# One column instead of sixteen products, first sums on TensorE, and a new order of loads and preparation pieces in an attention-and-FFN kernel

## The chip, the cores and the metric

The kernel runs on one core of one Trainium2 chip. The metric is the device time of one execution in microseconds. The kernel before took 1346.77 (median of 3 runs, 1346.31 to 1349.07).

## What is computed

A batch of 4 attentions over pooled keys, and a two-layer network on every token that comes out. The reference, cut:

```python
q: (4, 12288, 128) * 0.8;  kv: (4, 384, 32, 128) * 0.1;  w_sr: (128, 128)
kv_pool = kv.reshape(B, H//4, 4, W//4, 4, C).mean(axis=(2, 4))
k = v = kv_pool.reshape(B, -1, C) @ w_sr            # 768 keys per batch
a = softmax(q @ k.T / sqrt(C))
x = a @ v                                           # 49152 tokens
h = x @ w_in                                        # 128 -> 2048
out = (h - tanh(h)) @ w_out                         # 2048 -> 128
```

## The kernel before

The kernel uses that the softmax is close to uniform. With exp(s) - 1 - s as the small remainder of a score, the sum over keys is split into a straight part (products with the moment matrix Mh of the values) and the remainders' part. The network is expanded about the batch's centre: with h = h0 + d, h - tanh(h) is a value at h0, a slope times d, and terms of second and third order.

**Groups.** The 49152 tokens form 96 groups of 512 columns (24 groups a batch). `attention(g)` makes scores against 6 tiles of 128 keys, two at a time (L783, tile big), their exponentials (L787) and remainders r2 (L790, fp16, three tiles of 128x1024 a group). The three are summed: SP copies the first into rs (L802), POOL's two adding DMAs put the others on top (L805), and TensorE sums rs over the keys with a matrix of ones (`shares`, L809, into den). ACT turns this into the share t (L829). Numerator num: straight matmuls (L815) and values (L825). df = num * t (L836, DVE), its rounding dr (L839, POOL), the rest dl (L863, POOL). `feed_forward(g)` makes the 16 tiles of the first layer from dr (L894), on seven pairs ACT squares (L898) and DVE forms the cubes r (L901), on one pair ACT copies and POOL does the cubing (L905, L908, L912); `back` (L932) sums them with Wr, `straight` (L883) adds the slopes' product Ah, and ACT adds the value G0 as the bias (L943) and the result is stored.

**Preparation of a batch.** `keys(b)` makes pooled keys kvp: for batch 0 from 12 loads of 512 KB (L376) that DVE (L390) or POOL (L384) sum; for batches 1 to 3 by 16 DMAs, 15 of them adding DMAs of POOL (L362, "gather"), one for each group. Then the mean (row, L424 to L429), the centre (pc, L436, and col, L439), keys kTr, values vvr, the moment. `about_centre(b)` makes the first layer at the centre, four pieces `first(n)` of four matmuls (L535), the polynomial in hb (POOL for b > 0, DVE for b = 0), the scaled first-layer weights winr, `value(n)` (16 matmuls of one column, L595, summed into G0), `by_first(n)` (POOL, L697: output weights times slope) and `slopes(n)` (L701, 16 matmuls, summed into A, split into Ah), and `by_third(n)` (POOL, L714, weights Wr).

**Weights.** The weights arrive as 64-bit words. `words_of` loads 512 KB (L247 for w_in, L249 for w_out) and ACT (three operations) and DVE (four) turn them into 32 bits.

**What sets the order.** Every piece is an operation of `Plan` with a step, an engine, an estimated duration, and what it reads and writes. Plan.run places the operations one by one on the engine that is free first, smallest step first among those that can start; this is fixed when the program is built. Each engine, and SP's queue of loads, then runs its own list strictly in order. A name such as "held" that belongs to no tile only orders the planning; no semaphore comes of it. Steps are counted 8 to a group. The tables EARLY and LATER hold the steps between pieces of the preparation for batches 0 and 1 and for 2 and 3. Buffers per tag are in BUFS; the PSUM tags x (den, num and most of the preparation) and acc have one bank each, big three.

Of the kernel before, what the change touches and what calls it, by code (L numbers as in the profile page):

```python
# [11 lines left out]
F16 = mybir.dt.float16  # L12
# [144 lines left out]
def attention_then_ffn(ctx: ExitStack, tc: tile.TileContext, q, kv_by_key, kv_by_place, w_sr, w_in,  # L157
# [18 lines left out]

    BUFS = {"kc": 2, "kvp": 1, "kTr": 2, "vvr": 2, "Mn": 1, "Mh": 2, "A": 2, "Ah": 2, "Wg": 3, "Wr": 2,
            "winr": 2, "q": 4, "qr": 5, "ql": 2, "E": 2, "r2": 7, "rs": 3, "t": 2, "dl": 1, "df": 1, "dr": 2, "u": 3, "r": 4,
            "rp": 2, "v": 2, "z": 1, "o": 2, "row": 2, "col": 2, "G0": 2, "hb": 2, "W2": 1,
# [53 lines left out]
    def words_of(step, load_step, n, kind):  # L233
# [56 lines left out]
        plan.op(load_step, "SP", 0.5, load_words, (), (words,), late=2.0, dma=1.27)  # L290
# [8 lines left out]
    def weights(step, load_step, out_step, load_out):  # L299
# [3 lines left out]
        for n in range(NW):  # L303
            words_of(out_step + n / 8, load_out + n / 8, n, "o")
# [46 lines left out]
    def keys(b, s0):  # L351
# [17 lines left out]
        for j in range(0 if b else NK):  # L369
# [18 lines left out]
            else:  # L388
# [3 lines left out]
                plan.op(s, "DVE", 1.2, pool, (key,), ((kvp, j),))  # L392
# [8 lines left out]
        apart_by = (1, 6, 8, 8)[b]  # L401
# [98 lines left out]
    def about_centre(b, s0):  # L500

        cen, hb, G0, Am, Wr, winr = (f"{x}.{b}" for x in ("cen", "hb", "G0", "A", "Wr", "winr"))
        ph, pg, pa = (f"{x}.{b}" for x in ("ph", "pg", "pa"))
# [5 lines left out]
        sb(G0, "G0", [P, 1])  # L509
# [4 lines left out]
        FS, CS, AS, APART, SA, VA, TA, WI, WS = EARLY if b < 2 else LATER  # L514
# [4 lines left out]
        value_at = [known + VA + AS * n if b else n / 2 + VL for n in range(4)]  # L519
        third_at = [known + TA + AS * (n + 0.5) if b else n / 2 - THIRD for n in range(4)]  # L520
        for n in range(4):
            if b or n == 0:
                bank(f"{ph}.{n}", "x" if b else "acc", first_at[n])
            if b:
                bank(f"{pg}.{n}", "x", value_at[n])
                bank(f"{pa}.{n}", "x", slopes_at[n] + APART)
        if not b:
            bank(f"{pa}.0", "acc", slopes_at[0])
            bank(f"{pg}.0", "acc", value_at[0])
# [63 lines left out]
        def value(n):  # L593
            for f in range(4 * n, 4 * n + 4):
                PE.matmul(out=plan[f"{pg}.{n if b else 0}"][:, 0:1], lhsT=wout32[:, f],  # L595
                          rhs=x(3)[:, f : f + 1], start=(f % (4 if b else FT) == 0),
                          stop=(f % 4 == 3 and (b > 0 or n == 3)))

        def sum_value(n):
            if n:  # L600
                V.tensor_tensor(out=plan[G0], in0=plan[f"{pg}.{n}"][:, 0:1], in1=plan[G0], op=ALU.add)
            else:
                V.tensor_scalar(out=plan[G0], in0=plan[f"{pg}.{n}"][:, 0:1], scalar1=1.0,
                                scalar2=None, op0=ALU.mult)

# [20 lines left out]
        for n in range(4):  # L626
            plan.op(value_at[n], "PE", 0.9, partial(value, n), (gg, ("wout32", n)),
                    (f"{pg}.{n if b else 0}",), late=0.2)
            if b:
                plan.op(value_at[n], "DVE", 0.15, partial(sum_value, n), (f"{pg}.{n}",), (G0,))  # L630
        if not b:
            plan.op(value_at[3], "DVE", 0.15, partial(sum_value, 0), (f"{pg}.0",), (G0,))
# [28 lines left out]
        else:  # L661
            for j in range(2):
                pw = f"pw.{b}.{j}"
                big(pw, winr_at + j / 2)
                for k in range(2):
                    dg = f"dg.{b}.{j}.{k}"
                    sb(dg, "Wg", [P, FW, C], step=winr_at + j / 2 + k / 4)
                    fs = slice((2 * j + k) * FW, (2 * j + k + 1) * FW)

                    def diagonal(j=j, dg=dg, fs=fs):  # L670
                        by = x(8)[:, fs].unsqueeze(2).to_broadcast([P, FW, P])
                        of = ident.unsqueeze(1).to_broadcast([P, FW, P])
                        (PL if j else V).tensor_tensor(out=plan[dg], in0=of, in1=by, op=ALU.mult)

                    def scaled(j=j, k=k, dg=dg, pw=pw):
                        for n in range(FW):
                            f = (2 * j + k) * FW + n
                            at = (k * FW + n) * P
                            PE.matmul(out=plan[pw][:, at : at + P], lhsT=winT[:, f], rhs=plan[dg][:, n],
# [10 lines left out]
        for n in range(NW):  # L690
            wg = f"wg.{b}.{n}"
            fs = slice(n * FW, (n + 1) * FW)
            sb(wg, "Wg", [P, FW, C], step=slopes_at[n])

            def by_first(n=n, wg=wg, fs=fs):
                by = x(4)[:, fs].unsqueeze(2).to_broadcast([P, FW, C])
                PL.tensor_tensor(out=plan[wg], in0=wout32[:, fs], in1=by, op=ALU.mult)  # L697

            def slopes(n=n, wg=wg):
                for k in range(FW):  # L700
                    PE.matmul(out=plan[f"{pa}.{n if b else 0}"][:, 0:P], lhsT=winT[:, n * FW + k],  # L701
# [529 lines left out]
```

## Time and profile before

| | |
|---|---|
| median of 3 runs | 1346.77 us |
| profiled execution, span | 1346.26 us, 1344.5 us |
| busy TensorE matmul, DVE, ACT, POOL | 1279.7, 1221.3, 1195.9, 1147.4 us |
| granted TensorE clock, mean | 0.983 |
| first result of a group begins | 97.35 us |
| last result of a group begins | 1336.91 us |

Where a timeline row is quoted, its columns are start, duration, engine (with q where its sequencer issues a DMA), line, operation, out<-in, shape, count, and in brackets the idle time of the engine just before and what ended it. Rows of windows give the stretch, busy time of PE, PEld, DVE, ACT and POOL with the instructions in brackets, the granted clock, the DMA share and GB/s. Rows of groups end in busy us, mean ns of one, and idle time before. A float32 matmul stands as two records. Busy TensorE is not TensorE at its peak, since its ends are modelled.

### The profile page before, as it was taken

Reading aid. Unit: us, or ns where it says so; the run is one execution under the profiler, and the core shown is the slowest. Engines: PE = TensorE matmul, PEld = TensorE weight load, DVE = VectorE, ACT = ScalarE, POOL = GpSimd, SP = SyncE. Lnnn points to the kernel's source line nnn. Section 1 sums busy time; section 2 is a strip of 40 time slices with the busy share of each in tenths; the row PEclk is TensorE's granted clock in tenths of the full one; section 3 lists DMA queues with packets and bytes.
Section 4 is the critical chain, followed back from the end, with each engine's and each line's share of the span. In section 5 each row is a group of like instructions: output and inputs, shape, how many; then the busy total and the mean of one; then the engine's idle time right before and its main releaser. Section 6 shows DMA issues by size and latency. Waiting matters only on the chain.

```text
span 1344.5 us, 17619 instructions
## 1 busy us (share of the span) xinstructions
PE 1279.7 (95%) x5632; PEld 899.7 (67%) x5632; DVE 1221.3 (91%) x1214; ACT 1195.9 (89%) x1403; POOL 1147.4 (85%) x973
## 2 busy tenths in 40 slices
PE   2889999899999999999999999999999999999997
PEld 2657666577666667776666666777676667666664
DVE  6578999888899999998999999899999999899996
ACT  5378999888899999898999999889899999899995
POOL 2568999779999998799999998889998888798896
PEclk7989999999999999999999999999999999999999
DMA  8165666435566664444566664344444444444431
GB/s 345 46 122 119 139 140 132 104 98 135 125 130 138 141 131 109 99 118 107 128 139 132 138 141 114 95 105 109 110 101 104 117 104 102 101 102 106 114 85 35
DMA packets 83574, 160.07 MB, mean 119 GB/s; under 512 B 10032, under 2 KB 12208, under 8 KB 83472
## 3 DMA queue, kind: packets, MB, share of 16 engines
q0 software_dynamic: 34128, 68.04, 31.0%
q1 hardware_dynamic: 49344, 90.81, 19.3%
q8 instruction: 46, 0.75, 0.2%
q14 instruction: 56, 0.46, 0.1%
HBM read 57.93 MB, written 25.39 MB: 62 GB/s over the span
## 4 chain that ended last, share of the span: by engine, by line
PE 45%; POOL 39%; ACT 5%; issue 5%; DMA 3%; DVE 2%; SPq 0%; POOLq 0%; ACTq 0%; DVEq 0%
PE acc L932 13%; PE big L894 12%; POOL rp L912 9%; POOL z L912 9%; PE big L783 6%; POOL rs L805 5%; PE x L825 5%; POOL z L908 4%; POOL ql L819 3%; POOL dr L839 3%; ACT E L787 3%; PE x L815 2%; PE acc L883 2%; POOL dl L863 2%; DMA rs<-r 1%
## 5 line engine op out<-in xcount | busy, mean ns | idle before, releaser
L901 DVE SCALAR_TENSOR_TENSOR r<-big,u 128x1024 fp32r<-128x1024 f32 x672 | 780.6, 1218 | 33.6 <-ACT u L898 32.0
L898 ACT ACTIVATE u<-big 128x1024 f32<-128x1024 f32 x672 | 661.9, 1034 | 45.1 <-PE big L894 34.6
L894 PE MATMUL big<-dr,winr 128*128 128x512 f32 x1536 | 509.6, 413 | 2.5 <-DVE r L790 1.6
L932 PE MATMUL acc<-r,Wr 128*128 128x512 f32 x1344 | 424.7, 408 | 0.7 <-DVE r L901 0.7
L790 DVE SCALAR_TENSOR_TENSOR r<-E,big 128x1024 f16<-128x1024 f32 x288 | 350.3, 1218 | 47.9 <-ACT E L787 44.5
L894 PEld LDWEIGHTS big<-dr,winr 128*128 128x128 f32 x1536 | 275.3, 189 | 97.6 <-DVE r L790 23.1
L787 ACT ACTIVATE E<-big 128x1024 f32<-128x1024 f32 x288 | 295.8, 1029 | 18.7 <-PE big L783 11.4
L932 PEld LDWEIGHTS acc<-r,Wr 128*128 128x128 f32 x1344 | 251.6, 188 | 64.1 <-DVE r L901 1.6
L912 POOL TENSOR_TENSOR rp<-z,v 128x1024 fp32r<-128x1024 f32 x96 | 273.1, 2845 | 0.2
L912 POOL TENSOR_TENSOR z<-z,v 128x1024 f32<-128x1024 f32 x96 | 247.6, 2579 | 4.3
L805 POOL DMA_DIRECT2D rs<-r x192 | 226.4, 1179 | 11.6 <-DMA rs<-r 9.6
L783 PE MATMUL big<-qr,kTr 128*128 128x512 f32 x576 | 196.5, 424 | 1.6 <-ACT v L905 1.6
L839 POOL TENSOR_SCALAR dr<-df 128x512 fp32r<-128x512 f32 x96 | 68.7, 715 | 128.7 <-DVE df L836 92.6
L825 PE MATMUL x<-r,vvr 128*128 128x512 f16 x576 | 176.3, 389 | 0.0
L819 POOL TENSOR_TENSOR ql<-q,qr 128x512 fp32r<-128x512 f32 x96 | 165.0, 1719 | 0.0
L863 POOL TENSOR_TENSOR dl<-df,dr 128x512 fp32r<-128x512 f32 x96 | 164.2, 1711 | 0.0
L783 PEld LDWEIGHTS big<-qr,kTr 128*128 128x128 f32 x576 | 105.5, 190 | 42.9 <-DVE r L790 15.4
L908 POOL TENSOR_SCALAR z<-v 128x1024 f32<-128x1024 f32 x96 | 109.7, 1143 | 0.0
L905 ACT COPY v<-big 128x1024 f32<-128x1024 f32 x96 | 97.6, 1017 | 1.1 <-PE big L894 1.0
L943 ACT ACTIVATE o<-acc,G 128x512 f32<-128x512 f32 x96 | 65.7, 684 | 25.4 <-PE acc L932 24.3
L932 PE MATMUL acc<-rp,Wr 128*128 128x512 f32 x192 | 74.6, 469 | 13.9 <-POOL rp L912 10.1
L825 PEld LDWEIGHTS <-vvr 128*128 128x128 f16 x576 | 33.9, 99 | 79.5 <-issue 79.5
(183 smaller groups left out, 1023.4 us busy)
## 6 DMA issues: line engine op xcount, KB each, us to landing
rs<-r POOLq DMA_DIRECT2D x192, 256.0 KB, 3.9
q<-in_q_dram SPq DMA_DIRECT2D x96, 256.0 KB
rs<-r SPq DMA_DIRECT2D x96, 256.0 KB
out_dram<-o SPq DMA_DIRECT2D x96, 256.0 KB
kvp<-in_kv_by_place_dram POOLq DMA_DIRECT2D x45, 384.0 KB, 4.9
r<-in_kv_by_key_dram SPq DMA_DIRECT2D x6, 512.0 KB
kc<-inverse SPq DMA_DIRECT2D x12, 256.0 KB
u<-in_moe_w_in_dram SPq DMA_DIRECT2D x3, 512.0 KB
```

The lines of the kernel that those rows point to most:

```text
L783: PE.matmul(out=half(plan[s], h), lhsT=plan[kTr][:, n * P : (n + 1) * P], rhs=plan[qr], start=True, stop=True)
L787: A.activation(out=plan[e], in_=plan[s], func=AF.Exp)
L790: V.scalar_tensor_tensor(out=plan[r], in0=plan[e], scalar=-1.0, in1=plan[s], op0=ALU.add, op1=ALU.subtract)
L805: PL.dma_start(out=plan[rs], in_=plan[r2s[k]], accum_op=ALU.add)
L819: PL.tensor_tensor(out=plan[ql], in0=plan[qs], in1=plan[qr].bitcast(F32), op=ALU.subtract)
L825: PE.matmul(out=plan[num], lhsT=plan[vvr][:, n], rhs=half(plan[f"r2.{g}.{k}"], h), start=(start and h == 0), stop=(stop and h == 1))
L863: PL.tensor_tensor(out=plan[dl], in0=plan[df], in1=plan[dr].bitcast(F32), op=ALU.subtract)
L894: PE.matmul(out=half(plan[hp], h), lhsT=plan[winr][:, f * P : (f + 1) * P], rhs=plan[dr], start=True, stop=True)
L898: A.activation(out=plan[u], in_=plan[hp], func=AF.Square)
L901: V.scalar_tensor_tensor(out=plan[r], in0=plan[hp], scalar=1.0, in1=plan[u], op0=ALU.add, op1=ALU.mult)
L912: PL.tensor_tensor(out=plan[to], in0=plan[x], in1=plan[y], op=ALU.mult)
L932: PE.matmul(out=plan[acc], lhsT=plan[Wr][:, 2 * n + h], rhs=half(plan[r], h), start=(start and h == 0), stop=(stop and h == 1))
```

## The change

Four things change.

1. **Value as a column.** Output weights and first-layer weights change places in the slopes' products: POOL now scales winT by the slope (`by_first`) into a tile with one column more, ACT puts the value's factors into that column (`beside`), and the 16 slopes matmuls, now with the output weights as the stationary operand, give the transposed slopes and, in column 128, the value. `value` and `sum_value` go. A matmul with the identity (`turn_slopes`) turns the sum back, and ACT copies it twice instead of once.
2. **Groups 0 and 1** no longer copy and add their remainders by DMA: `shares` multiplies all three r2 tiles, six matmuls instead of two.
3. **Loads.** Loads of output weights and of the first q stand behind the last key loads ("held", written by the sum of key chunk 6).
4. **Places.** EARLY, LATER, MORE, KEYS1, ABOUT, ABOUT1, SL, SD, THIRD, PRO and `apart_by` of batch 1 change, which moves the preparation's pieces.

```diff
+    DIRECT, HELD = 2, 6
...
-        plan.op(load_step, "SP", 0.5, load_words, (), (words,), late=2.0, dma=1.27)
+        plan.op(load_step, "SP", 0.5, load_words, () if kind == "i" else ("held",), (words,), late=2.0,
+                dma=1.27)
...
-                plan.op(s, "DVE", 1.2, pool, (key,), ((kvp, j),))
+                plan.op(s, "DVE", 1.2, pool, (key,), ((kvp, j), "held") if j == HELD else ((kvp, j),))
...
-        apart_by = (1, 6, 8, 8)[b]
+        apart_by = (1, 5.3, 8, 8)[b]
...
-        sb(G0, "G0", [P, 1])
+        sb(At, "At", [P, C + 1])
...
-        def value(n):
-            for f in range(4 * n, 4 * n + 4):
-                PE.matmul(out=plan[f"{pg}.{n if b else 0}"][:, 0:1], lhsT=wout32[:, f],
-                          rhs=x(3)[:, f : f + 1], start=(f % (4 if b else FT) == 0),
-                          stop=(f % 4 == 3 and (b > 0 or n == 3)))
...
             def by_first(n=n, wg=wg, fs=fs):
                 by = x(4)[:, fs].unsqueeze(2).to_broadcast([P, FW, C])
-                PL.tensor_tensor(out=plan[wg], in0=wout32[:, fs], in1=by, op=ALU.mult)
+                PL.tensor_tensor(out=plan[wg][:, :, 0:C], in0=winT[:, fs], in1=by, op=ALU.mult)
+
+            def beside(wg=wg, fs=fs):
+                A.copy(out=plan[wg][:, :, C], in_=x(3)[:, fs])
 
             def slopes(n=n, wg=wg):
                 for k in range(FW):
-                    PE.matmul(out=plan[f"{pa}.{n if b else 0}"][:, 0:P], lhsT=winT[:, n * FW + k],
+                    PE.matmul(out=plan[f"{pa}.{n if b else 0}"][:, 0 : C + 1], lhsT=wout32[:, n * FW + k],
                               rhs=plan[wg][:, k], start=(k == 0 and (b > 0 or n == 0)),
                               stop=(k == FW - 1 and (b > 0 or n == 3)))
...
+        def turn_slopes():
+            PE.matmul(out=plan[pt][:, 0:P], lhsT=plan[At][:, 0:C], rhs=ident, start=True, stop=True)
+
         def upper_slopes():
+            A.copy(out=plan[Am], in_=plan[pt][:, 0:P])
             A.copy(out=plan[Ah][:, 0], in_=plan[Am])
...
         def shares():
-            for h in range(2):
-                PE.matmul(out=plan[den], lhsT=share, rhs=half(plan[rs], h), start=(h == 0),
-                          stop=(h == 1))
+            of = [rs] if g >= DIRECT else r2s
+            for n in range(2 * len(of)):
+                PE.matmul(out=plan[den], lhsT=share, rhs=half(plan[of[n // 2]], n % 2),
+                          start=(n == 0), stop=(n == 2 * len(of) - 1))
...
-    EARLY = (4, 1.6, 7, 3, 5, 4, 9, 18, 8)
-    LATER = (8, 8, 9, 7, 16, 8, 32, 28, 8)
-    MORE = 2.5
+    EARLY = (2, 4.4, 5, 3.5, 8, 15, 22, 8)
+    LATER = (4, 9, 9, 7, 16, 34, 31, 9)
+    MORE = 2
...
-            A.activation(out=plan[o], in_=plan[acc], func=AF.Identity, bias=plan[G0])
+            A.activation(out=plan[o], in_=plan[acc], func=AF.Identity, bias=plan[At][:, C : C + 1])
...
-    KEYS, ABOUT = 104, 100
-    KEYS1, ABOUT1 = 67, 57
+    KEYS, ABOUT = 104, 96
+    KEYS1, ABOUT1 = 61, 60
```

Three places show how the order moves. First SP's queue in the head, after the first nine key loads. Before:

```order
L376 DMA kc<-in_kv_by_key_dram 128x1024
L249 DMA u<-in_moe_w_out_dram 128x4x256
L249 DMA z<-in_moe_w_out_dram 128x4x256
L765 DMA q<-in_q_dram 128x512 x3
L249 DMA u<-in_moe_w_out_dram 128x4x256
L765 DMA q<-in_q_dram 128x512
L249 DMA u<-in_moe_w_out_dram 128x4x256
L376 DMA E<-in_kv_by_key_dram 128x1024
L376 DMA r<-in_kv_by_key_dram 128x1024 x2
```

Now (in_moe_w_out_dram are the output weights):

```order
L380 DMA kc<-in_kv_by_key_dram 128x1024
L380 DMA E<-in_kv_by_key_dram 128x1024
L380 DMA r<-in_kv_by_key_dram 128x1024 x2
L250 DMA u<-in_moe_w_out_dram 128x4x256 x3
L250 DMA z<-in_moe_w_out_dram 128x4x256
L756 DMA q<-in_q_dram 128x512 x5
```

The three key loads have moved ahead of four loads of output weights and four of q.

Second, TensorE between the scores and the values of group 0. Before:

```order
L701 MATMUL acc<-Wg,winT 128x128 x16
L809 LDWEIGHTS share
L809 MATMUL x<-rs,share 128x512
L809 LDWEIGHTS share
L809 MATMUL x<-rs,share 128x512
L815 MATMUL x<-qr,Mh 128x512 x2
```

Now the three remainder tiles (r_392, r_380, r_398) stand in the place of rs:

```order
L802 MATMUL x<-r_398,share 128x512
L802 LDWEIGHTS share
L802 MATMUL x<-r_398,share 128x512
L774 MATMUL big<-qr,kTr 128x512 x2
L685 MATMUL acc<-Wg,wout_69 128x129 x4
L808 MATMUL x<-qr,Mh 128x512 x2
```

All slopes stood ahead of the shares; now one quarter of the slopes does, the second follows the shares and the others stand among the values and the next scores.

Third, TensorE where batch 1's centre (from row) is made, at the end of group 12's work. Before:

```order
L932 MATMUL acc<-r,Wr 128x512 x2
L894 MATMUL big<-dr,winr 128x512 x2
L436 MATMUL x<-row,wsr 128x1
L815 MATMUL x<-qr,Mh 128x512 x2
L815 MATMUL x<-ql,Mh 128x512
L783 MATMUL big<-qr,kTr 128x512 x2
```

Now:

```order
L889 MATMUL big<-dr,winr 128x512 x2
L440 MATMUL x<-row,wsr 128x1
L927 MATMUL acc<-r,Wr 128x512 x2
L536 MATMUL x<-col,win_67 128x1 x4
L889 MATMUL big<-dr,winr 128x512 x2
```

The centre now stands one group of attention's matmuls later, and the first quarter of the first layer follows at once, three more within the next group.

More of the change, by code (lines that the diff above doesn't have):

```diff
@@ L297, in words_of, with out_weights, weights @@
         plan.op(step, "DVE", 0.66, add, (part, rs), (part,), port=True)
-    def weights(step, load_step, out_step, load_out):
+    def out_weights(step, load_step):
+        for n in range(F // WN):
+            words_of(step + n / 8, load_step + n / 8, n, "o")
+    def weights(step, load_step):
         NW = F // WN
@@ L625, in about_centre @@
             plan.op(s0 - 5, on, 1.1, third_order, (hb,), (hb, a3s))
[L626 to L632, printed above, removed]
         NW, FW = 4, FT // 4
@@ L705, in sum_slopes @@
             def sum_slopes(n=n):
-                of = plan[f"{pa}.{n}"][:, 0:P]
+                of = plan[f"{pa}.{n}"][:, 0 : C + 1]
                 if n:
-                    V.tensor_tensor(out=plan[Am], in0=of, in1=plan[Am], op=ALU.add)
+                    V.tensor_tensor(out=plan[At], in0=of, in1=plan[At], op=ALU.add)
                 else:
-                    A.copy(out=plan[Am], in_=of)
+                    A.copy(out=plan[At], in_=of)
             def by_third(n=n, fs=fs):
@@ L733, in about_centre @@
         joined = slopes_at[3] + (APART if b else 1) + 0.1
-        plan.op(joined, "ACT", 0.3, upper_slopes, (Am,), (Ah,), late=0.1)
+        bank(pt, "x" if b else "acc", joined)
+        plan.op(joined, "PE", 0.25, turn_slopes, (At, "ident"), (pt,), late=0.2)
+        plan.op(joined, "ACT", 0.65, upper_slopes, (pt,), (Am, Ah), late=0.1)
         plan.op(joined, "POOL", 0.35, lower_slopes, (Am, Ah), (Ah,))
@@ L770, in attention @@
         ago = math.floor(BUFS["q"] - (AT["lower_q"] - AT["added"][0]) / UN)
-        behind = (f"first.{g - ago}",) if g >= ago + 3 else ()
+        behind = ("held",) if g < ago + 3 else (f"first.{g - ago}",)
         plan.op(s0 + AT["rounded_q"] - 7, "SP", 0.5, load_q, behind, (qs,), late=2.0, dma=0.65)
@@ L1150, in attention_then_ffn @@
     start(-LEAD - 80)
-    weights(-LEAD - 50, -LEAD - 60, -17.7, -LEAD - 46)
+    weights(-LEAD - 50, -LEAD - 60)
+    plan.tile("held", "held", 1, lambda: None)
     GATHER = (24, 30, 30)
-    KEYS, ABOUT = 104, 100
-    KEYS1, ABOUT1 = 67, 57
+    KEYS, ABOUT = 104, 96
+    KEYS1, ABOUT1 = 61, 60
     SL = 6
-    VL = -10
-    SD = 0.5
-    THIRD = 36
-    PRO = (2, 0, 0)
+    SD = 0
+    THIRD = 20
+    PRO = (5, 0, 0)
     for b in range(B):
```

61 lines of the change are left out of this document (28 added, 33 removed).

## The prediction

> **What bounds the kernel now.** I read the page first, then the result rows of ACT (one per group) to cut the run into stretches, then the timeline of the first 80 us, then groups and windows of the stretches that are not steady.
>
> ```profile
> span 1344.5 us, 17619 instructions
> DVE  6578999888899999998999999899999999899996
> ...
> 97.35 0.69 ACT L943 ACTIVATE o<-acc,G 128x512 f32<-128x512 f32 x1
> 201.89 0.69 ACT L943 ACTIVATE o<-acc,G 128x512 f32<-128x512 f32 x1 [0.26 <-PE acc L932]
> 239.63 0.69 ACT L943 ACTIVATE o<-acc,G 128x512 f32<-128x512 f32 x1 [0.23 <-PE acc L932]
> 257.68 0.69 ACT L943 ACTIVATE o<-acc,G 128x512 f32<-128x512 f32 x1 [0.30 <-PE acc L932]
> 389.34 0.69 ACT L943 ACTIVATE o<-acc,G 128x512 f32<-128x512 f32 x1 [0.76 <-PE acc L932]
> 514.90 0.68 ACT L943 ACTIVATE o<-acc,G 128x512 f32<-128x512 f32 x1
> 668.75 0.68 ACT L943 ACTIVATE o<-acc,G 128x512 f32<-128x512 f32 x1
> 832.00 0.68 ACT L943 ACTIVATE o<-acc,G 128x512 f32<-128x512 f32 x1
> 983.76 0.68 ACT L943 ACTIVATE o<-acc,G 128x512 f32<-128x512 f32 x1
> 996.05 0.68 ACT L943 ACTIVATE o<-acc,G 128x512 f32<-128x512 f32 x1
> ```
>
> These are the results of groups 0, 8, 11, 12, 21, 31, 42, 55, 66 and 67. Groups 8 to 11 take (239.63 - 201.89) / 3 = 12.58 us each: the steady beat, with DVE near 9 tenths in most slices. The rest is loss. The first result comes at 97.35. Groups 12 to 21, where batch 1 is prepared, take 149.7 us for ten: 23.9 more than ten beats. Groups 32 to 42 (batch 2) lose 153.85 - 11 x 12.58 = 15.5, groups 56 to 66 (batch 3) 151.76 - 138.4 = 13.4. No steady group's instructions change place, as the order shows, so the prediction is about four stretches: the head and three preparations. The profiled execution took 1346.26 (span 1344.5 and 1.8 around it), 0.5 under the median of the runs, 1346.77; my sum starts from 1346.3.
>
> **Head, first part: the last key loads.**
>
> ```profile
> 30.00:32.00 2.00, 0.70 (x1) 0.50 (x2) 1.93 (x2) 1.97 (x4) 0.00 (x0) 0.50 0.78 317
> 32.00:34.00 2.00, 2.00 (x4) 0.68 (x3) 0.64 (x2) 0.26 (x1) 1.36 (x2) 0.50 0.00 0
> ...
> q<-in_q_dram SPq DMA_DIRECT2D x96, 256.0 KB
> u<-in_moe_w_out_dram SPq DMA_DIRECT2D x3, 512.0 KB
> ...
> 17.87 2.33 DVE L390 TENSOR_REDUCE kvp<-r 128x64 f32<-128x1024 f32 x2
> 22.06 0.33 SPq L376 DMA_DIRECT2D E<-in_kv_by_key_dram  x1
> 23.46 0.97 SPq L376 DMA_DIRECT2D r<-in_kv_by_key_dram  x2
> 32.56 2.52 POOL L384 TENSOR_TENSOR r<-r 128x512 f32<-128x512 f32 x3 [9.96 <-DVE kvp L390]
> 38.11 3.73 PE L535 MATMUL acc<-col,win 128*128 128x1 f32 x32 [0.25 <-DVE col L439]
> ```
>
> The windows' last two columns are DMA share and GB/s: the DMA is full until it runs dry at about 31.6 us. The last three key loads go out last, behind four loads of output weights (512 KB each) and four of q (256 KB each); the fold at 32.56 starts when they are in. In the new order of SP those eight stand behind. They are 4 x 0.524 + 4 x 0.262 = 3.15 MB; the DMA's mean rate from 4 us on is about (12 key, 8 weight loads of 0.524 and 4 of 0.262 = 11.5 MB) / 28 us = 0.41 MB/us. So the last key comes **7.7 us** earlier, and the chain fold, mean, centre, first layer (38.11 now, about 30.4 then) moves with it. The buffers allow it: the last of the three needs the tile that the first of the two sums at 17.87 lets go, at 19.0, and the 13 loads ahead keep the DMA at work until about 4 + 13 x 0.524 / 0.41 = 20.6. What it costs: the output weights' own pieces (four DVE operations each) now fall among the chain, in front of a diagonal and a remainder; about 0.4 us. They were hidden in the DMA wait before.
>
> **Head, second part: remainders of groups 0 and 1 summed by TensorE.**
>
> ```profile
> 54.83 2.35 DVE L790 SCALAR_TENSOR_TENSOR r<-E,big 128x1024 f16<-128x1024 f32 x2 [0.60 <-ACT E L787]
> 65.36 0.88 POOL L805 DMA_DIRECT2D rs<-r  x1 [2.63 <-DMA rs<-r]
> 68.78 1.01 PE L809 MATMUL x<-rs,share 128*128 128x512 f16 x2 [7.25 <-DMA rs<-r]
> 70.48 1.22 PE L815 MATMUL x<-qr,Mh 128*128 128x512 f32 x2 [0.69 <-ACT t L829]
> 71.94 2.78 PE L825 MATMUL x<-r,vvr 128*128 128x512 f16 x6
> 74.83 0.69 DVE L836 TENSOR_TENSOR df<-x,t 128x512 f32<-128x512 f32 x1 [13.12 <-PE x L825]
> 85.92 0.60 PE L825 MATMUL x<-r,vvr 128*128 128x512 f16 x2
> ...
> 40.00:60.00 20.00, 19.89 (x141) 17.98 (x141) 11.77 (x31) 10.71 (x14) 11.02 (x12) 0.91 0.10 34
> 60.00:80.00 20.00, 10.51 (x36) 5.71 (x36) 5.68 (x6) 6.07 (x10) 9.04 (x11) 0.73 0.60 117
> ```
>
> The third remainder of group 0 is ready at 54.83 + 2.35 = 57.18. A copy and two adding DMAs of POOL follow one another, TensorE idles 7.25 us, and df comes at 74.83, 17.65 us after the remainder. Without the DMAs, TensorE does in that interval: a quarter of the slopes (1.1 by the row of L701 below), six share matmuls (0.30 each at full clock: 1.8; 0.50 each as at 68.78: 3.0), ACT's 0.6 for the share, two more quarters of the slopes (2.2), three straight matmuls (1.1 to 1.85) and six value matmuls (1.8 as at 85.92, 2.78 as at 71.94). That is 8.6 at full clock, 11.5 at the lower one. I take 8.6, because TensorE then runs on without the hole: it is busy 19.89 of 20 us at 40 to 60 with a granted 0.91, against 0.73 where it idles. The gain is **9.0** (6.1 at the low clock).
>
> The Trainium skill, page "TensorE: Matmul & The Clock Gate", Part 1, has the clock fall to half after an idle window of some 3.4 us and come back after as long a busy one. By that rule the hole costs more than itself and the sum is the 9.0; without it, 6.1. The 0.50 beside the idle stretch at 30 us agrees.
>
> New in this stretch is ACT's second copy of the slopes and their rounding between scores and squares of group 0: with TensorE's turn and four extra share matmuls of group 1 (1.2 us), I put the start of group 0's squares 0.7 later. Past this point DVE has work without a break in both kernels. Head together: 7.7 - 0.4 + 9.0 - 0.7 = **15.6** (10 to 18). POOL is no bound here by my count: its adds for groups 0 and 1 (0.9 each at 65.36) are gone, and its ten pieces (diagonals, slopes, cubic weights), at the 1.5 us of L697 below, fill 15 of the 21 us between 37 and 58.
>
> **Preparations of batches 1 to 3.**
>
> ```profile
> 252.71 0.35 PE L436 MATMUL x<-row,wsr 128*128 128x1 f32 x2 [3.00 <-DVE row L429]
> 257.41 1.22 DVE L790 SCALAR_TENSOR_TENSOR r<-E,big 128x1024 f16<-128x1024 f32 x1 [3.65 <-ACT E L787]
> ...
> 340.00:360.00 20.00, 19.30 (x92) 13.80 (x90) 17.11 (x19) 17.04 (x21) 20.00 (x17) 1.00 0.63 125
> 540.00:560.00 20.00, 20.00 (x97) 14.24 (x96) 18.84 (x19) 18.25 (x23) 13.93 (x11) 1.00 0.43 110
> ...
> L701 PE MATMUL x<-Wg,winT 128*128 128x128 f32 x32 | 4.3, 277 | 0.0
> L595 PE MATMUL x<-hb,wout 128*128 128x1 f32 x32 | 4.0, 246 | 0.1
> L342 PE MATMUL x<-Mn 128*128 128x128 f32 x2 | 0.4, 272 | 0.0
> L708 DVE TENSOR_TENSOR A<-x,A 128x128 f32<-128x128 f32 x3 | 0.8, 281 | 0.0
> L655 POOL TENSOR_TENSOR winr<-win,kc 128x512 fp32r<-128x512 f32 x4 | 8.8, 2190 | 0.0
> L697 POOL TENSOR_TENSOR Wg<-wout,hb 128x512 f32<-128x512 f32 x4 | 6.0, 1494 | 0.0
> ```
>
> The groups are those of batch 2 (515 to 669 us). Two rows matter first. The value products (L595) cost TensorE 4.0 us per batch though they make one column: 32 records of 246 ns, against 277 for 128 columns. As column 129 of the slopes they are nearly free (4.3 x 129/128). Added are one turn (two records as L342: 0.4), ACT's extra copy (under 0.3) and four copies of 128x4: not in the trace, between nothing (off the path) and the 0.28 of a 128x128 piece on DVE, 0.2 taken, beside other work. Net on TensorE: **-3.6 per batch**. Removed with them are four rounds of the one-bank tile x, which DVE had to empty each time.
>
> Batches 2 and 3: TensorE fills 540 to 560 (20.00), so the 3.6 counts; later POOL's pieces (L655, L697) bind, and the order draws those apart (L697 in four groups instead of three). I take 2.8 each, 0 to 4.5.
>
> Batch 1: group 12 took 257.68 - 239.63 = 18.05, 5.5 above the beat. TensorE reached the centre 3.0 us before DVE had the mean, everything behind it in order stood, and DVE lost 3.65 at 257.41. In the new order the centre stands about 40 matmuls later, the mean after one piece of sums done earlier: I count 4.5 of the 5.5 as gone. Of the 3.6 I count 2, as POOL is full there (20.00 of 20 at 340). Together **6.5**, 1 to 12. What is late next: three quarters of the first layer now stand within one group, and DVE's copy of each must release x; that puts 4 to 6 us of TensorE into one group, which I hold already in the remaining loss.
>
> **Sum:** 1346.3 - 15.6 - 6.5 - 2 x 2.8 = 1346.3 - 27.7 = **1318.6**.
>
> **Rivals.** (1) *The keys come no earlier.* The loads are held by their place in SP's queue, nothing else waits; with up to eight loads in flight, later ones may share the DMA with the last keys. Against: at present arrival follows issue order (the last keys, issued last, end the full stretch). It takes the 7.7 away: 1326. Chance 0.10.
> The Trainium skill, page "DMA: Bandwidth & Descriptors", section "Queues, rings and completion order", says that each DMA engine takes the descriptors of one ring in ring order; by that the keys stay ahead, as in the forecast. The trace agrees only as far as the last loads end last.
> (2) *POOL becomes the bound.* In the head its quarters of the cubic weights wait for output weights that now land last, and rounding of df stands behind them in its queue; from about 58 us, when df comes, any lateness is paid in full: 5 us. In batches 1 to 3 a full POOL (20.00 at 340) leaves half of what I count there, 6 of 12. Gain 16.6: 1330. Chance 0.11.
> (3) *Slower: the beat locks longer.* Groups 0 and 1 now hand over to the DMA sums at group 2, and if group after group POOL's adds then come later than TensorE's shares, each pays. The beat does depend on POOL: 12.58 with the gather in its queue, 996.05 - 983.76 = 12.29 without. It decides from 27.7 / 84 steady groups = 0.33 us; at 0.4 the gain is turned into 1346.3 - 27.7 + 33.6 = 1352. Against: the beat is the same after the head and after batch 1's preparation, which it enters differently. Chance 0.03.
>
> **Chances.** Forecast 0.74, rivals 0.10, 0.11 and 0.03, all gains used up by POOL and x 0.02. About 0.2% (2.7 us) is what a measurement of this kernel can tell from no change: faster 0.95, within it 0.02, slower 0.03. The forecast's bounds add to gains of 11 to 39. All terms at their poorest at once is the part left out, so the range is 13 to 39: 1307 to 1333, with rivals 1 and 2 inside it.
>
> **What would show it.** Head: first layer near 30.4; no idle of TensorE over 2 us between 45 and 60; df of group 0 near 58.5; first result near 82. Batch 1: group 12 near 13 us, no wait of TensorE at the centre. Batches 2 and 3: no L595, loss 12 to 13 and 10 to 11 us. Wrong if the beat is not 12.58, if DVE waits at the first layer's copies, or if POOL's adds of group 2 hold its queue until df of group 1.

## The result

The changed kernel takes **1312.73 us** (median of 4 runs, 1312.45 to 1314.71) beside 1346.54 for the kernel before (median of 4, 1345.14 to 1349.07): ratio **0.9752**, 95% interval 0.9736 to 0.9767, or 33.4 us less (31.4 to 35.5). The prediction was 1318.6, 5.9 too high, in a range of 1307 to 1333. All four stretches came out within the bounds given for them (batch 2 at the edge): the head near the forecast, batches 1 to 3 with more, and by another mechanism than the one I priced.

The profiled execution of the changed kernel took 1312.51 us, span 1310.7. The page's head and its slices (tenths busy), and the result rows of the same ten groups as before (0, 8, 11, 12, 21, 31, 42, 55, 66, 67):

```profile
span 1310.7 us, 17375 instructions
PE   5899999999999999999999999999999999999997
...
82.33 0.69 ACT L938 ACTIVATE o<-acc,At 128x512 f32<-128x512 f32 x1
186.82 0.69 ACT L938 ACTIVATE o<-acc,At 128x512 f32<-128x512 f32 x1 [0.26 <-PE acc L927]
224.46 0.69 ACT L938 ACTIVATE o<-acc,At 128x512 f32<-128x512 f32 x1 [0.24 <-PE acc L927]
237.03 0.69 ACT L938 ACTIVATE o<-acc,At 128x512 f32<-128x512 f32 x1 [0.24 <-PE acc L927]
364.84 0.69 ACT L938 ACTIVATE o<-acc,At 128x512 f32<-128x512 f32 x1 [0.26 <-PE acc L927]
490.29 0.68 ACT L938 ACTIVATE o<-acc,At 128x512 f32<-128x512 f32 x1
639.62 0.69 ACT L938 ACTIVATE o<-acc,At 128x512 f32<-128x512 f32 x1 [0.23 <-PE acc L927]
802.70 0.68 ACT L938 ACTIVATE o<-acc,At 128x512 f32<-128x512 f32 x1
950.93 0.68 ACT L938 ACTIVATE o<-acc,At 128x512 f32<-128x512 f32 x1
963.17 0.68 ACT L938 ACTIVATE o<-acc,At 128x512 f32<-128x512 f32 x1
```

Groups 8 to 11 still take (224.46 - 186.82) / 3 = 12.55 us: the beat has not changed. I go on taking 12.58 for it, so that losses compare with those of the prediction.

| stretch | before | after | gain | forecast |
|---|---|---|---|---|
| first result | 97.35 | 82.33 | 15.0 | 15.6 |
| group 12 | 18.05 | 12.57 | | |
| loss of batch 1's preparation (groups 12 to 21) | 23.9 | 14.6 | 9.3 | 6.5 |
| loss of batch 2's (32 to 42) | 15.5 | 11.0 | 4.5 | 2.8 |
| loss of batch 3's (56 to 66) | 13.4 | 9.9 | 3.5 | 2.8 |

Together 32.3 us. The last result begins 32.7 us earlier (1336.91 to 1304.18), so nothing of size lies outside these rows.

The head, from the timeline of the changed kernel: the fold that needs the last keys, the first layer, scores, POOL's two slopes products, a DVE piece of the output weights, the second and third remainder of group 0, the shares, df, and then windows of TensorE's clock.

```profile
24.77 2.54 POOL L388 TENSOR_TENSOR r<-r 128x512 f32<-128x512 f32 x3 [1.92 <-DVE kvp L394]
30.53 3.73 PE L536 MATMUL acc<-col,win 128*128 128x1 f32 x32 [0.25 <-DVE col L443]
44.96 0.71 PE L774 MATMUL big<-qr,kTr 128*128 128x512 f32 x2
46.33 0.74 PE L774 MATMUL big<-qr,kTr 128*128 128x512 f32 x2 [0.66 <-ACT winr L668]
46.36 2.26 POOL L678 TENSOR_TENSOR Wg<-winT,hb 128x512 f32<-128x512 f32 x2
46.55 2.37 DVE L272 TENSOR_SCALAR v<-v 128x512 int32<-128x512 int32 x1
48.69 1.22 PE L774 MATMUL big<-qr,kTr 128*128 128x512 f32 x2 [1.62 <-ACT qr L759]
49.17 2.34 DVE L781 SCALAR_TENSOR_TENSOR r<-E,big 128x1024 f16<-128x1024 f32 x2
53.17 2.42 PE L802 MATMUL x<-r,share 128*128 128x512 f16 x6
59.88 0.69 DVE L829 TENSOR_TENSOR df<-x,t 128x512 f32<-128x512 f32 x1 [0.89 <-PE x L818]
...
46.00:48.00 2.00, 0.74 (x2) 0.30 (x2) 2.00 (x2) 2.00 (x3) 2.00 (x3) 1.00 0.43 40
50.00:52.00 2.00, 1.57 (x5) 1.38 (x6) 2.00 (x3) 1.33 (x2) 0.00 (x0) 0.50 0.00 0
52.00:54.00 2.00, 2.00 (x9) 1.41 (x9) 2.00 (x4) 0.80 (x2) 0.87 (x1) 0.50 0.00 0
```

The fold is 7.8 us earlier than before, the first layer 7.58 (30.53 against 38.11). The third remainder ends at 49.17 + 2.34 = 51.51; df comes 8.37 later, where before it came 17.65 later. Two things are new. The DVE piece L272 lasted 2.37 us beside POOL's products, and remainders two and three stand behind it. And TensorE's clock is 0.50 from 50 to 54 (in windows of 1 us it falls between 48 and 49 and is back between 55 and 56), though TensorE's longest single hole there is the 1.62 before 48.69.

The head's chain thus has four links. The first layer comes 7.58 earlier; from there to the end of the third remainder it takes 1.91 longer (19.07 before, 20.98 now); from the remainder to df 9.28 less; from df to the first result 22.45 instead of 22.52, the same.

### The profile page after: what moved, and what is told of

It reads as the page before. It is cut to its first block, busy times and chain, and to the rows that moved or that the text cites. A ratio compares the mean times of both kernels' runs of the same rounds, so it can differ in the third digit from the quotient of the medians.

```text
span 1310.7 us, 17375 instructions
## 1 busy us (share of the span) xinstructions
PE 1267.8 (97%) x5520; PEld 888.8 (68%) x5520; DVE 1221.1 (93%) x1201; ACT 1196.2 (91%) x1423; POOL 1142.7 (87%) x969
## 3 DMA queue, kind: packets, MB, share of 16 engines
q0 software_dynamic: 33552, 66.99, 31.4%
## 4 chain that ended last, share of the span: by engine, by line
PE 42%; POOL 40%; ACT 8%; issue 5%; DVE 3%; DMA 2%; POOLq 0%; SPq 0%; ACTq 0%; DVEq 0%
PE acc L927 12%; PE big L889 11%; POOL rp L907 10%; POOL z L907 10%; POOL rs L797 5%; PE big L774 5%; PE x L818 4%; POOL z L903 4%; ACT E L778 4%; POOL dr L832 3%; POOL ql L812 3%; PE acc L878 2%; PE x L808 2%; ACT v L900 2%; ACT o L938 2%
## 5 line engine op out<-in xcount | busy, mean ns | idle before, releaser
L797 POOL DMA_DIRECT2D rs<-r x188 | 222.0, 1181 | 5.9 <-DVE r L896 3.3
L938 ACT ACTIVATE o<-acc,At 128x512 f32<-128x512 f32 x96 | 65.7, 684 | 21.6 <-PE acc L927 21.4
```

The source lines that it names most:

```text
L797: PL.dma_start(out=plan[rs], in_=plan[r2s[k]], accum_op=ALU.add)
```

## The experiments

Twelve runs were made on several chips (one of them is the changed kernel again), each beside the kernel before; its medians there were 1347.7 to 1349.3, so I compare by ratio, and turn a ratio into time with 1346.5. "First result" and losses are from each run's own trace.

How much such trace values scatter must be known first. In four kernels whose preparations of batches 2 and 3 are those of before (before itself and the runs with loads, direct shares and centre alone) batch 2 lost 15.5, 14.6, 13.9 and 14.7, batch 3 13.4 to 13.8. So against the mean of batch 2, 14.7, the change gains 3.7 there rather than 4.5. In batch 1 the old places lost 23.9, 23.9 and 24.7 (before, loads, direct shares). Of six kernels with the column and the new places five lost 10.9 to 11.1 in batch 2, and one 12.3. The first layer of one and the same head came at 38.1 to 38.7. The run with the centre alone executes the head in the order of before, and its first result came at 99.05, 1.7 later: 0.6 of this stands at the first layer, and from 57 to 60 its clock was 0.50 where before had 1.00. So a difference of less than 2 us between two first results is not a finding.

### One part alone

**Loads alone.**

```diff
-plan.op(load_step, "SP", 0.5, load_words, (), (words,), ...)
+plan.op(load_step, "SP", 0.5, load_words, () if kind == "i" else ("held",), (words,), ...)
```

> The kernel before with one part of the change alone: the loads of output weights and the first loads of q stand behind the seventh key sum. Theory: the last key loads arrive 7.7 us earlier, the first layer starts near 30.5 (before 38.11), the chain behind it moves with it, 0.4 us go to the output weights' pieces in front of it: median 7.3 under the kernel before (ratio 0.9946). Rival 1 of the prediction (later loads share the DMA with the last keys): first layer stays near 38, ratio 1.000. A second rival: the keys come early, but the head's later steps are held by output weights that now land last: first layer near 30.5, first result less than 4 us earlier, ratio above 0.997.

Measured: ratio 0.9944 (0.9925 to 0.9963), 7.5 us (5.0 to 10.1). First layer at 30.86, 7.25 earlier; first result at 93.07, only 4.3 earlier. So rival 1 of the prediction falls, the keys come early. What takes part of it back in this trace, from its timeline:

```profile
57.27 0.69 DVE L288 CUSTOM_DVE_ANT_0 wout<-wout,o 128x1024 uint16<-128x1024 uint16 x1
58.02 1.86 PE L599 MATMUL acc<-hb,wout 128*128 128x1 f32 x8 [4.36 <-DVE wout L288]
60.23 6.69 PE L705 MATMUL acc<-Wg,winT 128*128 128x128 f32 x32 [0.34 <-DVE G L607]
```

The value products now wait 4.36 us for the last output weights, and the slopes behind them take 6.69 us (3.73 before), at a clock of 0.50 from 50 to 66. So the trace shows what the second rival says, nearly in size. The median does not: its 7.5 us are the theory's 7.3, and the interval excludes the rival's ratio of 0.997. The profiled execution, 1341.13, was slower than the median by 1.5; which of the two is nearer stays open.

**Direct shares alone** (the edit told in words).

```diff
-matmuls of rs with share, behind the copy and two adding DMAs
+for g < 2: matmuls of all three r2 tiles with share, no copy, no DMA
```

> The kernel before with another part alone: the remainders of groups 0 and 1 are summed by TensorE instead of the copy and two adding DMAs. Theory: the 7.25 us hole of TensorE goes and its clock stays up: df of group 0 9.0 us earlier (74.83 before, near 66), first result near 88.4, ratio 0.9933. Rival: the clock stays low: 6.1 us, ratio 0.9955. Second rival: something else, found late in the head, takes the place of the DMAs: under 3 us, ratio above 0.998.

Measured: ratio 0.993 (0.9912 to 0.9948), 9.4 us; first result at 89.08 (8.3 earlier), df at 65.65. From its timeline:

```profile
55.33 2.35 DVE L791 SCALAR_TENSOR_TENSOR r<-E,big 128x1024 f16<-128x1024 f32 x2 [0.61 <-ACT E L788]
58.30 1.47 PE L812 MATMUL x<-r,share 128*128 128x512 f16 x6
65.65 0.69 DVE L839 TENSOR_TENSOR df<-x,t 128x512 f32<-128x512 f32 x1 [3.45 <-PE x L828]
```

From the third remainder's end (57.68) to df: 7.97 us, 9.7 less than before, with the six shares at 0.25 us each. The theory holds: TensorE stayed at work and its clock up (1.00 in every window from 52 to 64).

**Column alone**, at the old places (the edit cut, in part told in words).

```diff
-value(n): 16 matmuls of one column, summed into G0
+rhs=plan[wg][:, k] of 129 columns; G0 = At[:, C]; turn_slopes
```

> The kernel before with G0 as a column of the slopes' products alone, at the old places of the preparations' pieces. Theory of the prediction: 3.6 us of TensorE saved per preparation, of which 2 count in batch 1 and 2.8 in each of batches 2 and 3; losses against the beat: batch 1 23.9 to near 22, batch 2 15.5 to near 12.7, batch 3 13.4 to near 10.6; median 7.6 lower, ratio 0.9944. Rival: POOL sets the pace of the preparations, the saved matmuls lie beside it and the gain in batches 2 and 3 belongs to the new places: each loss falls by under 1 us, ratio 0.998 to 1.000.

Measured: ratio 0.995 (0.9934 to 0.9967), 6.7 us (4.4 to 8.9); in the trace the last result is 4.1 earlier. First result at 95.37, 2.0 earlier, which I had not forecast; that is hardly more than the scatter. Losses 23.9, 14.5, 11.9: nothing in batch 1, within the scatter in batch 2, 1.5 in batch 3. So the median is near the theory's 7.6, but the losses are the rival's in batches 1 and 2: what the theory placed there did not come there.

**Centre alone**, three numbers of batch 1.

```diff
-apart_by = (1, 6, 8, 8)[b]      KEYS1, ABOUT1 = 67, 57
+apart_by = (1, 5.3, 8, 8)[b]    KEYS1, ABOUT1 = 61, 60
```

> The kernel before with two places moved alone: batch 1's key steps 6 later, apart by 5.3 instead of 6, and what follows the centre 3 earlier (the numbers of the change), the tables of batch 2 and 3 as before. Theory: the stall of group 12 (18.05 us, 5.5 over the beat) is one wait of TensorE for the mean and goes: group 12 near 13.5, loss of batch 1 from 23.9 to near 19.4, median 4.5 lower, ratio 0.9967. Rival: the pieces only move, and what group 12 no longer loses comes back in groups 13 to 21: group 12 near 13, loss of batch 1 still above 22, ratio 0.999 to 1.000.

Measured: ratio 0.9978 (0.9968 to 0.9988), 3.0 us. Group 12 is at the beat (12.58), the loss of batch 1 falls from 23.9 to 21.3. So 5.5 go in group 12 and 2.8 come back behind it (group 16 alone takes 17.40, before 14.97): between theory and rival.

### One part taken out of the change

**The changed kernel with the old order of loads.**

```diff
-() if kind == "i" else ("held",)
+()
```

> The changed kernel without its new order of loads (output weights and q wait for nothing). Theory: first layer back near 38, first result near 90, 7.3 us over the changed kernel's 1312.73: 1320. Rival: the gains of the head overlap (with the shares on TensorE the chain from the keys no longer decides): under 4 us, below 1317.

Measured: ratio 0.9819 (0.9803 to 0.9834), 9.0 us over the changed kernel's ratio. First layer at 38.91, first result at 92.66, 10.3 later. The rival (overlapping gains, under 4 us) falls. With the old order, TensorE waits for ACT's rounding of the next q (L759), which stands on ACT behind group 0's third exponentials; the last of q's first loads had been issued at 26.5:

```profile
57.98 2.07 PE L774 MATMUL big<-qr,kTr 128*128 128x512 f32 x4 [3.08 <-ACT qr L759]
...
58.00:60.00 2.00, 2.00 (x5) 1.29 (x6) 0.68 (x1) 0.79 (x2) 1.93 (x2) 0.50 0.90 163
62.00:64.00 2.00, 2.00 (x8) 1.71 (x7) 0.65 (x1) 1.07 (x2) 0.00 (x0) 0.50 0.00 0
```

There is a hole of 3.08 us in front of the scores, and a clock of 0.50 from between 57 and 58 until 64. In the changed kernel the hole at this place is 1.62; its clock is low for about as long (48 to 55), but less of that falls behind the third remainder. From the end of the third remainder to df it is 10.73 us here (58.67 to 69.40) against 8.37.

**The changed kernel with copy and adding DMAs for groups 0 and 1.**

```diff
-DIRECT, HELD = 2, 6
+DIRECT, HELD = 0, 6
```

> The changed kernel with the remainders of groups 0 and 1 summed by the copy and the adding DMAs again. The changed kernel's trace gives 15.0 us for the head, of which 7.6 stand at the first layer, so 7.4 at the shares. Theory: those 7.4, no more: 1320, first result near 89.7. Rival: the 9.0 of the prediction was right, and what is missing was lost elsewhere in the head: 1321.7, first result near 91.3.

Measured: ratio 0.9813 (0.9797 to 0.9828), 8.2 us over; first result at 90.20, 7.9 later. Between the two expectations; it doesn't tell them apart.

**The changed kernel with the old tables** (EARLY, LATER, and the three numbers of the centre, which the cut leaves out; ABOUT, MORE, SD, THIRD and PRO stay as changed).

```diff
-EARLY = (2, 4.4, 5, 3.5, 8, 15, 22, 8)     LATER = (4, 9, 9, 7, 16, 34, 31, 9)
+EARLY = (4, 1.6, 7, 3, 5, 9, 18, 8)        LATER = (8, 8, 9, 7, 16, 32, 28, 8)
```

> The changed kernel with the old places of the preparations' pieces (tables and the two numbers of batch 1 as before, without the entry of the value products). The changed kernel's trace gives gains of 9.3, 4.5 and 3.5 us in batches 1, 2 and 3. Theory of the prediction (2 of batch 1 and 2.8 each of the others belong to the column): the places are worth 7.3, 1.7 and 0.7: 9.7 over the changed kernel, 1322.4. Rival: the column is worth nothing at the old places because POOL binds: 17 over, 1330. Second rival: the places are worth nothing beyond the centre of group 12: 4.5 over, 1317.2.

Measured: ratio 0.9863 (0.9847 to 0.9879), 14.9 us over the changed kernel's ratio. Losses 23.9, 14.0 and 11.6. The rival was right for batch 1: at the old places the column is worth nothing there, though everything else of the change is in. Its 17 us were too many because batches 2 and 3 lost less than before.

### Column and places: the fourth corner

**All places, but value products again**, and **column and centre without the tables**.

```diff
-EARLY = (2, 4.4, 5, 3.5, 8, 15, 22, 8)
+EARLY = (2, 4.4, 5, 3.5, 8, 7, 15, 22, 8)
-rhs=plan[wg][:, k]
+rhs=x(3)[:, f : f + 1]
```

> The changed kernel with all its places, but with the value products as matmuls of one column again. With the column alone on the old places measured (losses 23.9, 14.5 and 11.9 against 23.9, 15.5 and 13.4 before) and both together 14.6, 10.9 and 9.9, this is the fourth corner. Theory A (the places make the gain and the column only saves a little beside them): losses near 15, 12 and 11, time 2 to 4 us over the changed kernel. Theory B (they need each other: without the column TensorE and the one-bank tile have no room for the denser places): losses near 18 to 24, 14 and 13, time 9 to 14 us over the changed kernel.

> The kernel before with the column and the two numbers of batch 1's centre, on the old tables. The column alone gave nothing in batch 1 (23.94), the centre alone 2.7 (21.26, group 12 at the beat but group 16 at 17.40). Theory: what came back after the centre alone is TensorE's work crowding into groups 14 to 18, from which the column takes 3.6 us: loss of batch 1 near 17.7. Rival: what came back is POOL's and the places' (the table for batch 1): the loss stays above 20, and the rest of the 9.3 belongs to the table.

For these two and the next two the changed kernel ran again, on the same chip:

> The changed kernel unaltered, beside the other three on one chip, so that they can be compared with it. Expected: ratio 0.9752 to the kernel before, first result near 82.3, losses of the three preparations 14.6, 10.9 and 9.9 us.

It gave 1311.68 (median of 5), ratio 0.9741 (0.9727 to 0.9756), losses 14.6, 11.0 and 10.0, first result at 81.42.

The places without the column: 1320.34, ratio 0.9794 (0.9779 to 0.9809), **8.7 us over the changed kernel beside it**: just under the range of theory B, far over that of theory A. Column and centre without the tables: ratio 0.993 (0.9915 to 0.9945), batch 1's loss 23.0; the rival was right, the table (EARLY) makes the larger part of batch 1's gain.

| loss of preparations 1, 2, 3 | old places | new places |
|---|---|---|
| value products | 23.9, 15.5, 13.4 | 17.7, 13.1, 11.9 |
| column | 23.9, 14.5, 11.9 | 14.6, 11.0, 9.9 |

Why they need each other is to be read in the windows over batch 1's preparation (groups 12 to 21), in this order: before, column alone, places without column, changed. Columns are the stretch, then busy time of PE, PEld, DVE, ACT, POOL:

```profile
239.63:389.35 149.72, 141.13 (x649) 100.95 (x648) 127.49 (x136) 125.00 (x148) 131.98 (x124) 0.99 0.52 117
```

```profile
237.71:387.45 149.74, 138.77 (x619) 97.41 (x618) 126.94 (x132) 126.17 (x153) 132.03 (x124) 0.99 0.51 117
```

```profile
224.73:368.25 143.52, 141.00 (x649) 100.75 (x648) 127.37 (x135) 124.94 (x147) 131.66 (x124) 0.99 0.52 122
```

```profile
224.46:364.84 140.38, 135.92 (x619) 96.78 (x618) 127.01 (x131) 125.09 (x152) 131.79 (x124) 1.00 0.55 124
```

At the old places TensorE idles 149.72 - 141.13 = 8.6 us. The column takes 2.4 us of its work, and the idle time grows to 11.0: nobody had waited for that work. With the new places alone the idle time is 2.5 us, with the same 141 us of work. There the column counts: 5.1 us fewer busy, 3.1 us shorter, 4.5 idle. POOL does the same 132 us in every row, and by the whole stretch it looks as if it never were the bound. But the bound changes within the stretch. Groups 13 to 16 and groups 17 to 21 apart, the same four kernels in the same order:

```profile
257.68:318.12 60.44, 59.76 (x287) 42.85 (x286) 51.00 (x54) 50.94 (x62) 46.83 (x55) 1.00 0.42 105
318.12:389.34 71.22, 67.06 (x309) 48.41 (x308) 62.52 (x62) 61.02 (x71) 71.22 (x59) 1.00 0.59 128
...
255.22:316.25 61.03, 59.62 (x279) 42.13 (x279) 50.98 (x53) 51.35 (x63) 46.89 (x55) 0.99 0.41 104
316.25:387.45 71.20, 65.34 (x287) 45.86 (x286) 61.64 (x59) 61.78 (x75) 71.20 (x59) 1.00 0.59 128
...
237.29:302.75 65.46, 63.38 (x313) 46.64 (x312) 54.17 (x67) 51.91 (x63) 59.00 (x67) 0.98 0.44 109
302.75:368.25 65.50, 65.16 (x285) 45.56 (x285) 61.02 (x58) 60.92 (x71) 61.16 (x50) 0.99 0.58 131
...
237.03:297.59 60.56, 59.30 (x289) 43.42 (x288) 53.29 (x63) 51.97 (x67) 54.10 (x63) 1.00 0.45 109
297.59:364.84 67.25, 64.14 (x279) 44.81 (x278) 61.53 (x57) 61.01 (x73) 66.18 (x54) 1.00 0.62 136
```

Before, TensorE is full in groups 13 to 16 (59.76 of 60.44), and POOL in groups 17 to 21: 71.22 of 71.22 us, while TensorE idles 4.2. The value products run there from 307 to 351 us, mostly in POOL's full part. So the column alone leaves that part as long as it was, 71.20 with POOL at 71.20, and TensorE only idles more. The new places bring work of POOL forward (59.0 and 54.1 us of it lie in groups 13 to 16, before 46.8), and groups 17 to 21 get shorter, 65.5 and 67.3. But they bring the value products forward too, to 277 to 310, where TensorE is the bound: without the column groups 13 to 16 take 65.5 us, with it 60.6. So the places relieve POOL's part of the stretch and the column TensorE's, and 1.8 of the column's 4.9 us are given back behind it, where POOL is nearly full again (66.18 of 67.25). That it is POOL's pieces in the tables that do this is read from the rows; no run moved them alone. Over batch 2 TensorE idles 3.9 us before, 1.9 with the places alone, 2.2 with both; that stretch is not taken apart here.

### The DVE piece beside POOL

**Six weights' pieces held** until group 0's third remainder.

```diff
+        if kind == "o" and n >= 2:
+            plan.later += [len(plan.ops), len(plan.ops) + 1]
```

> The changed kernel with DVE's first two pieces (integer maximum and shift) of the output weights 2 to 7 held until group 0's third remainder is done. In the changed kernel one of these, of 0.43 us elsewhere, lasted 2.37 us in front of a remainder while POOL multiplied slopes, and df of group 0 came at 59.88 instead of 58.3 to 58.5. Theory: those pieces stood ahead of the remainders and their stretching cost 1.5 to 1.9 us: third remainder ends near 49.6 instead of 51.51, df near 58.2, first result near 80.6, median 1.6 us lower. Rival: the pieces are paid behind the remainders instead (POOL's cubic weights wait for them, and df's rounding stands behind these): df near 58.2 but first result within 0.5 of 82.33, no gain. Second rival: the remainders wait for something else: third remainder within 0.4 of 51.51.

Measured: ratio 0.9719 (0.9705 to 0.9732). The planner also put ACT's second copy of winr ahead of the first remainder's exponentials, so the first remainder came at 47.32 instead of 45.41, and the third ended 21.1 us after the first layer, as in the changed kernel (21.0). It tells nothing of the mechanism. The first result at 81.32 is 1.0 earlier than in the changed kernel, with a first layer 0.7 earlier (29.80). Its ratio is 0.0033 under the changed kernel's first and 0.0022 under its second (0.9741, above), 3.0 to 4.4 us, of which its trace shows under 1 us; what makes the rest stays open.

**Only the pieces between the remainders held.**

```diff
+plan.later += [len(plan.ops) + 2 + i for i in ((1,) if n == 2 else (0, 1))] if kind == "o" and n in (2, 3) else []
```

These are the shift of output weight 2 and both pieces of weight 3.

> The changed kernel with only those one-operand pieces of output weights 2 and 3 held that DVE has between the first and the second remainder of group 0 (the shift of 2, both of 3); the first remainder keeps its place, which it did not in the run that held six of the eight weights' pieces. Theory: DVE's piece waited for POOL's two slopes products, 46.36 to 48.62, and that alone made remainders two and three late: third remainder ends near 49.6 (51.51 in the changed kernel), df near 58.3, first result 1.0 to 1.9 earlier, ratio to the changed kernel 0.9988. Rival: the third and fourth quarter of the slopes on TensorE, which stand ahead of df's last matmuls, now wait for output weights that come 2 to 3 us later: third remainder near 49.6, df within 0.5 of 59.9 or later, no gain. Second rival: the remainders wait for something else: third remainder within 0.4 of 51.5.

Measured: 1309.19 (median of 5) beside 1311.68, ratio 0.9716 (0.9703 to 0.9729) against 0.9741 (0.9727 to 0.9756). Its timeline:

```profile
31.22 0.27 PE L536 MATMUL acc<-col,win 128*128 128x1 f32 x1 [0.25 <-DVE col L443]
...
47.03 3.26 POOL L678 TENSOR_TENSOR Wg<-winT,hb 128x512 f32<-128x512 f32 x3
47.91 2.35 DVE L781 SCALAR_TENSOR_TENSOR r<-E,big 128x1024 f16<-128x1024 f32 x2 [0.61 <-ACT E L778]
53.93 0.59 DVE L272 TENSOR_SCALAR v<-v 128x512 int32<-128x512 int32 x1
58.77 0.68 DVE L829 TENSOR_TENSOR df<-x,t 128x512 f32<-128x512 f32 x1
81.43 0.69 ACT L938 ACTIVATE o<-acc,At 128x512 f32<-128x512 f32 x1 [0.44 <-PE acc L927]
```

Here the first layer came 0.7 later than in the changed kernel's first profile and 1.1 later than in its second, so I count from it. The third remainder ends 50.26 - 31.22 = 19.0 us after it, against 21.0 in both profiles: **2.0 us earlier, as the theory said.** The first result comes 50.2 us after it, against 51.8 and 51.3: 1.1 to 1.6 us of the 2.0 arrive. Counted from the start of the execution nothing arrives in this trace beside the second run (81.43 against 81.42), since the first layer was late. The median is 2.5 us under the changed kernel's, but the two intervals overlap by 0.0002, so that it beats the changed kernel is likely and not settled; from the run before it (0.9719) it cannot be told apart.

## Why the prediction was right, and where it wasn't

**The last key loads: right.** -7.7 was forecast at the first layer, -7.58 measured. The keys' early arrival needs no more than the order of SP's queue.

**The shares on TensorE: the size right, the reason half wrong.** From third remainder to df 8.6 us were forecast, 8.37 measured (9.28 gained against 9.0). But I wrote that this holds "because TensorE then runs on without the hole" at full clock, and the clock was 0.50 between 50 and 54; the six shares took 2.42 us instead of the 1.47 of the run with direct shares alone. Up to the end of the shares (55.59) it took 4.08 us where I had counted 2.9. What made up for it lies behind: 4.29 us where I had counted 5.7, because ACT's 0.6 lay beside scores and a slopes quarter, and slopes, straight matmuls and values followed without a gap at a clock of 1.00. That the sum came out is in part luck.

The Trainium skill, page "TensorE: Matmul & The Clock Gate", Part 1, speaks of an idle window of about 3.4 us before the clock halves. By the rows above, the longest hole was 1.62 us. From the end of the scores at 44.96 + 0.71 = 45.67 to 48.69 TensorE worked 0.74 us of 3.02, and the clock fell. So here the rule read as "no hole over 3.4 us" does not hold; the measurement decides: a stretch of some 3 us that is mostly idle was enough.

It is not always enough, and not always needed. In the run with column and centre TensorE stood still for 3.08 us (53.76 to 56.84), and its clock was 1.00 in every window until 64; with the old order of loads a hole of the same 3.08 us came with a clock of 0.50 until 64. With the centre alone the clock fell to 0.50 at 57, though TensorE is recorded busy without a gap from 50 to 60. In the second run of the changed kernel it was low only from 50 to 54. So what sets the clock is not shown here, and one trace is not a rule.

**The term that I mis-sized in the head** is the 0.4 for output-weight pieces in front of the chain. From first layer to the end of the third remainder the head lost 1.91. The last experiment moves three DVE pieces and leaves 19.04 of 20.98, so all of it belongs to these pieces, of which one waited for POOL; the rest of what I had named there cost nothing in sum. I had looked at how much each engine has to do, not at which two engines' pieces cannot run at the same time. The 0.7 for ACT's copies and TensorE's turn did not come either: from df to the first result nothing changed. So that the head's 15.0 stands so near 15.6 is luck in part: 1.5 too much lost in one place, 0.8 less than counted in another, and 0.3 more from the shares.

**The loads and the shares: perhaps not a sum.** At the first result the loads bring 4.3 us alone and 10.3 when they are taken out of the change, the shares 8.3 and 7.9. The first difference is larger than the scatter of heads (1.7), but by the medians the loads are worth 7.5 (5.0 to 10.1) and 9.0 (6 to 12 by the two intervals), which are not told apart. In the traces the late output weights hold the value products for 4.36 us ahead of the slopes when the loads stand alone; in the changed kernel there are no value products, and three of the slopes' quarters stand behind the shares. That the column is the part which makes the loads pay more is argued from these rows; loads and column alone were not run together.

**Batch 1: right in sign, wrong in step.** I wrote "I count 4.5 of the 5.5 as gone" for the centre and "of the 3.6 I count 2" for the column. The stall did go, but alone it brought 2.7, the column alone 0, both 0.9 (loss 23.0), and with the table 9.3. The failed step is that both terms were priced each by itself and the table, which moves all the other pieces, was given no term. That "POOL is full there (20.00 at 340)" was read rightly: at the old places POOL has no idle moment in groups 17 to 21. But then the 2 should have been 0 there, and what was worth most was to ask which pieces could leave the full part. The table does that, and once it does, the column's matmuls lie where TensorE is the bound and 3.1 us of them count. The 3.6 itself was measured as 2.4 us of busy time at the old places and 5.1 at the new ones.

**Batches 2 and 3: sizes low.** 2.8 each was forecast, 3.7 to 4.5 and 3.5 measured. That the saved work would count because TensorE fills its windows was right for the new places only: at the old ones the column brought up to 1 and 1.5.

**The rivals.** (1) fell, with the first layer at 30.5. (2) fell as a forecast: batches 1 to 3 gained 17.3 instead of 6, though POOL still is the bound of a part of them. (3) fell: the beat is 12.55. Its threshold had been counted with 84 groups; outside the head and the three preparations there are 63, so that it decides from 0.44 us a group. Of the tests that I had named, the first layer, the first result, group 12 and the beat came as written, and TensorE had no single hole over 2 us between 45 and 60. df at 58.5 was missed by 1.4 (the DVE piece), and the losses of batches 2 and 3, 12 to 13 and 10 to 11, by 1.0 and 0.1 on the good side.

## What to carry to other kernels

Work taken from an engine counts only where that engine is the bound. Subtract busy from length for each engine, and do it part by part: over 150 us POOL was busy 132 and looked free, over the last 71 it had no idle moment. Where the bound changes within a stretch, an edit of the order and an edit of the work have to be priced together, since neither need be worth its price alone. And when a piece moves in time, ask also which piece of another engine it will then run beside.

## What the hardware showed unexpectedly

DVE's pieces with one SBUF input (L269, L272, 128x512) lasted 0.41 to 0.43 us in all but one of the sixteen times in the changed kernel. The exception began at 46.55, 0.19 after POOL's first slopes product, and ended at 48.92, 0.3 after the second one had ended at 48.62; so it looks as if it did nothing until both were done. DVE's remainders, which read PSUM (tile big), are not held up: with the pieces moved away, two of them took 2.35 us at 47.91, their usual time, beside POOL's three products (47.03 to 50.29). In the second run of the changed kernel the 2.37 us came again, and in the run with the old tables too. In the run without direct shares such a piece met a single POOL piece of 1.51 us and lasted 1.77; moved behind the remainders, in the last experiment, it lasted 0.59, begun 0.31 before a POOL product ended. In all five cases it ended 0.28 to 0.30 us after POOL's piece.

```profile
L272 DVE TENSOR_SCALAR v<-v 128x512 int32<-128x512 int32 x8 | 5.3, 665 | 0.1
L269 DVE TENSOR_SCALAR v<-v 128x512 f32<-128x512 f32 x8 | 3.4, 419 | 5.0 <-ACT v L266 5.0
```

In the groups of the changed kernel the mean of L272 is 665 ns against 419 for L269: one of eight times of 2.37 does that, (2370 + 7 x 422) / 8 = 665.

The Trainium skill, page "SBUF — State Buffer", section "SBUF: two separate sides", calls the port pair that VectorE and GpSimd share an exclusive lock, for a VectorE operation in a 2-port mode or with two SBUF inputs: who starts first holds it for the whole instruction, and the other blocks. The trace agrees (that L272, with one SBUF input, ran in such a mode is not shown by any row), with one addition: POOL's second product, queued behind the first, went ahead of DVE's piece, which by the records had begun at 46.55.
